# Attention-times-V in a fused transformer block: 16 tokens x 8 key offsets on the partitions, N=16 indicator sums, weights re-laid out through DRAM

## The chip, the cores and the metric

One core of a Trainium2 chip. The metric is the device time of the whole kernel in microseconds (us); the state of an execution (fast or slow) comes from its time and clock. PE is the tensor engine, DVE the vector engine, ACT the scalar engine, POOL the GpSimd engine; SP is the engine that issues the DMAs. "The Trainium skill" is the set of notes on the chip that is cited by page title.

## The reference, cut to what matters

A transformer block with conditioned layer norms: attention with 32 heads of 16 over eight dilated keys per token, then a gated FFN. 2,048 tokens of 512 features, bf16.

```python
W, dil = (8, 2)
idx = pos[:, None] - (jnp.arange(W) * dil)[None, :]     # keys s, s-2, ..., s-14
mask = idx >= 0
...
attn = _softmax(logits, axis=-1)                        # [head, token, 8]
o = jnp.einsum('bhsw,bhswd->bhsd', attn, vg)            # the AV product
...
x = x + ga * _A_ref(h, A_wqkv, A_wo)
h = _layernorm(x, axis=-1) * (1 + cb) + sb
x = x + gb * _B_ref(h, B_w1, B_w3, B_w2)
```

## The kernel before: the parts that matter

The program lists operations with dependences and priorities; a list scheduler with fixed cost guesses lays them out on the engines before the kernel is built, and semaphores are put in afterwards. So every change of the graph can change the order everywhere. There are 16 token tiles of 128 tokens, in four chunks of four. Per tile, attention forms q*k for eight offsets on DVE (128x4096), sums it over the head dimension on PE (32 matmuls of N=32), takes a softmax, multiplies V by it on DVE (128x4096) and sums over the offsets on PE:

```python
# V of the eight offsets, token s on partition s, offset w in the free dimension: one DMA
p.dma(lambda: vv.at[:], bass.AP(v_dram, T * P * D, [[D, P], [-2 * D, W], [1, D]]), ...)
def av(e):   # DVE: in place, attention weights straight from SBUF
    a_w = bass.AP(ve.at[0], 0, [[W * H, P], [H, W], [0, DH], [1, H]])
    v_w = bass.AP(vv.at, 0, [[W * D, P], [D, W], [H, DH], [1, H]])
    return e.tensor_tensor(v_w, v_w, a_w, ALU.mult)
def acc(e):  # PE: transposing sum over the 8 offsets, 4 feature blocks x 8 offsets, N = 128
    for ft in range(KT):
        for w in range(W):
            ins = e.matmul(b[:, ft * P:(ft + 1) * P], vv.at[:, w, ft * P:(ft + 1) * P], ident[:],
                           start=(w == 0), stop=(w == W - 1))
```

Token tile 0 has keys before the start of the sequence. It is handled by zeroing two buffers on POOL, by eight partial products and by seven small memsets:

```python
p.op("pool", lambda e: e.memset(vpq0.at[:], 0.0), 3600, -7e5, w=[vpq0])     # 128x4096
p.op("pool", lambda e: e.memset(vvsh0.at[:], 0.0), 3600, -7e5, w=[vvsh0])   # 128x4096
```

Of the kernel before, what the change touches and what calls it, by code (L numbers as in the profile page):

```python
# [7 lines left out]
ACT = mybir.ActivationFunctionType  # L8
# [3 lines left out]
P = 128  # L12
# [10 lines left out]
NCH = S // 512  # L23
EPS = 1e-5
# [36 lines left out]
class Op:  # L61
    __slots__ = ("eng", "fn", "cost", "pr", "deps", "vals", "n", "start", "end", "seen", "pos", "dma", "bytes",
                 "waits", "inc", "clock", "raw", "prev")

    def __init__(self, eng, fn, cost, pr):
        self.eng, self.fn, self.cost, self.pr = eng, fn, cost, pr
        self.deps = {}
        self.vals = []
        self.prev = []
        self.end = None  # L70
        self.dma = False
        self.bytes = 0
        self.inc = None


class Program:
# [37 lines left out]
    def dma(self, out, in_, pr, nbytes, r=(), w=(), part=(), after=(), eng="sp", cost=450):  # L114
# [8 lines left out]
        return self.op(eng, fn, cost, pr, r=r, w=w, part=part, after=after, dma=nbytes)  # L123
# [83 lines left out]
    def synchronize(self):  # L207
        known = {e: {} for e in ENGINES}
        waited = set()
        for o in self.placed:  # L210
            e = o.eng
            need = {}
            for d, true in list(o.deps.items()) + [(d, False) for d in o.prev]:
                if d.dma:
                    need[("dma", d.n)] = d
# [7 lines left out]
            for key, d in todo:  # L223
# [5 lines left out]
                for k, x in d.clock.items():  # L229
                    if have.get(k, 0) < x:  # L230
                        have[k] = x
# [5 lines left out]
        count = {e: 0 for e in ENGINES}  # L237
        for o in self.placed:
            if o.dma:
                o.inc = (self.ctx.enter_context(self.nc.semaphore(f"d{o.n}")), 16, 16)  # L240
# [47 lines left out]
def _build(p, A_x, A_wqkv, A_wo, B_w1, B_w3, B_w2, c, w_mod, out):  # L288
# [15 lines left out]
    kT = sb([P, KT, S], bf, "kT")  # L304
# [4 lines left out]
    vshb = [sb([P, W, D], bf, f"vsh{i}") for i in range(3)]  # L309
    pqb = [sb([P, W, KT, P], bf, f"pq{i}") for i in range(2)]  # L310
    osb = [sb([P, D], bf, f"o{i}") for i in range(2)]
    atb = [sb([P, W, H], bf, f"attn{i}") for i in range(2)]
    exb = [sb([P, W, H], f32, f"ex{i}") for i in range(2)]
# [3 lines left out]
    csb = sb([P, KT, P], bf, "csb")  # L317
    ident = sb([P, P], bf, "ident")
    E_sb = sb([P, KT, H], bf, "E")
    ones = sb([P, P], bf, "ones")  # L320
    cst = sb([P, 2], f32, "cst")
# [24 lines left out]
    wm_s = [at([P, KT, 1024], bf, f"wm_s{i}", 12288 * i) for i in range(2)]  # L346
    wm_g = [at([P, KT, 512], bf, f"wm_g{i}", 12288 * i + 8192) for i in range(2)]

    v_dram = nc.dram_tensor("v_scratch_dram", (S, D), bf)
# [13 lines left out]
    smpool = Pool("sm", [(atb[i], exb[i], i) for i in range(2)])  # L363
    otpool = Pool("ot", otb)
# [17 lines left out]
    vpq0 = Val("pq", pqpool)  # L382
    vvsh0 = Val("vsh", vshpool)
# [13 lines left out]
    p.op("pool", lambda e: e.memset(vpq0.at[:], 0.0), 3600, -7e5, w=[vpq0])  # L397
    p.op("pool", lambda e: e.memset(vvsh0.at[:], 0.0), 3600, -7e5, w=[vvsh0])
# [5 lines left out]
    vx = [Val(f"x{T}") for T in range(NT)]  # L404
    for T in range(4):
# [144 lines left out]
    def proj_qk(cch, kind, vh, pr):  # L550
        dstv = Val("q", qpool) if kind == 0 else Val("k")
        for ft in range(KT):
# [10 lines left out]
            def ev(e, ft=ft, vp=vp):  # L563
                if kind == 0:
                    return e.activation(dstv.at[:, ft, :], bank(vp), ACT.Copy, scale=SCALE)
                return e.activation(kT[:, ft, 512 * cch:512 * cch + 512], bank(vp), ACT.Copy)
# [4 lines left out]
    def proj_v(T, vh, pr):  # L571
# [19 lines left out]
        p.dma(v_dram[T * P:(T + 1) * P, :], lambda: vt.at[:], pr, 131072, r=[vt], w=[vd], cost=400)  # L591
# [5 lines left out]
    def attention(T, pr):  # L597
        cch = T // 4
        tt = T % 4
        ks = [vk[cch]] + ([vk[cch - 1]] if tt == 0 and T else [])  # L600
        if T == 0:
            vp = vpq0
            for w in range(W):
                def prod(e, w=w):
                    n = P - 2 * w
                    in0 = bass.AP(vq[0].at, 2 * w, [[KT * 512, P], [512, KT], [1, n]])
                    in1 = bass.AP(kT, 0, [[KT * S, P], [S, KT], [1, n]])
                    o = bass.AP(vp.at, w * KT * P + 2 * w, [[W * KT * P, P], [P, KT], [1, n]])
                    return e.tensor_tensor(o, in0, in1, ALU.mult)

                p.op("dve", prod, 400, pr, r=[vq[0]] + ks + ([vp] if w == 0 else []), part=[vp])
        else:
            vp = Val("pq", pqpool)

            def prod(e):
                in0 = bass.AP(vq[cch].at, tt * P, [[KT * 512, P], [0, W], [512, KT], [1, P]])
# [188 lines left out]
```

## Time and profile before

| | before |
|---|---|
| median | 295.06 us of 3 runs; 295.28 of 4 beside the changed kernel |
| span of the profiled execution | 295.4 us (a run of 297.19, slower than the median) |
| first QKV matmul | 16.47 us |
| first FFN matmul | 103.30 us |
| from there to the end | 192.1 us |

Busy time by engine (page, first part): us, share of the span, instructions.

```profile
PE 262.3 (89%) x2120; PEld 144.8 (49%) x2152; DVE 216.9 (73%) x369; ACT 134.5 (46%) x228; POOL 32.2 (11%) x60
```

The groups of the AV product (page, groups by line): partitions x elements, type, count | busy us, mean ns of one | idle just before. L665 is the DVE product, L674 the sums of N=128 on PE, L627 the logit sums of N=32.

```profile
L665 DVE TENSOR_TENSOR sb_vsh<-sb_vsh,sb_attn 128x4096 bf16<-128x4096 bf16 x16 | 36.5, 2284 | 0.0
...
L674 PE MATMUL pall<-sb_ident,sb_vsh 128*128 128x128 bf16 x512 | 31.2, 219 | 1.0 <-DVE sb_vsh L665 1.0
...
L627 PE MATMUL pall<-sb_E,sb_pq 128*128 128x32 bf16 x512 | 15.0, 177 | 2.0 <-DVE sb_pq L618 1.6
```

The two sums have equally many matmuls and weight loads, and busy time 31.2 against 15.0 us. (The mean of one matmul overlaps with its neighbours: divide busy time by the count.)

The table by stretches, cut at the first FFN matmul. Columns: stretch and length, then busy us (instructions) for PE, weight load, DVE, ACT, POOL; then granted clock, DMA share, GB/s.

```profile
core 0: us, PE busy (x) PEld busy (x) DVE busy (x) ACT busy (x) POOL busy (x), PEclk, DMA share, GB/s
0.00:103.30 103.30, 80.44 (x869) 48.95 (x881) 84.22 (x147) 50.59 (x86) 20.88 (x38) 0.95 0.74 233
103.30:295.40 192.10, 181.84 (x1251) 95.85 (x1272) 132.69 (x223) 83.90 (x143) 11.30 (x22) 0.98 0.16 52
```

In the second stretch PE is busy 95% of the time. In the first, DVE and PE are both at about 80%. The chain of waits is the work that ended last, followed back step by step. The chain over the whole span, and one burst of 32 AV sums in it:

```profile
PE 69%; DVE 21%; ACT 4%; issue 2%; POOL 2%; DMA 1%; DVEq 0%
...
110.34 1.79 PE pall L674 x32
```

DMA issues (page, last part): KB each and median us from issue to landing.

```profile
sb_vsh<-v_scratch_dram SPq DMA_DIRECT2D x15, 1024.0 KB, 5.1
...
out_dram<-sb_o SPq DMA_DIRECT2D x16, 128.0 KB, 1.7
```

### The profile page before, as it was taken

The page shows a single profiled execution, that of the slowest core. Times are in us where ns is not written, and L with a number is a line of the kernel's source. Part 1 is how long each engine was busy: PE and PEld are TensorE (multiplying, and loading weights), DVE is VectorE, ACT ScalarE, POOL GpSimd, SP SyncE. Part 2 cuts the span into 40 slices and gives each one's busy share as a digit, 9 for nine tenths or more (in the row PEclk, how much of TensorE's full clock was granted, in tenths as well). Part 3 has the DMA queues.
Part 4 walks back from the last instruction along what each step waited for, and adds up shares of the span by engine and source line. Part 5 has one row for each costly group of instructions (what it writes and reads, how often), then busy time and mean ns, then how long its engine had stood idle before and what let it go on. Part 6 is the DMA issues. An engine that isn't in the chain of part 4 may idle for free.

```text
span 295.4 us, 5127 instructions
## 1 busy us (share of the span) xinstructions
PE 262.3 (89%) x2120; PEld 144.8 (49%) x2152; DVE 216.9 (73%) x369; ACT 134.5 (46%) x228; POOL 32.2 (11%) x60
## 2 busy tenths in 40 slices
PE   0479996699999699999999999699999989999796
PEld 0324645357757345556545647355546634444342
DVE  4763988968999969989648997977588851366611
ACT  2146751654643645677105564140564570376500
POOL 8610001010311110010000010103100000000000
PEclk9999998599999979999999999799999999999999
DMA  5999994267726814124410040333000001100001
GB/s 180 360 287 359 335 294 163 87 204 215 241 85 197 254 50 145 43 100 143 161 36 20 2 142 11 133 81 118 18 2 1 2 0 36 38 0 0 0 20 53
DMA packets 34255, 34.10 MB, mean 115 GB/s; under 512 B 1775, under 2 KB 33207, under 8 KB 34231
## 3 DMA queue, kind: packets, MB, share of 16 engines
q1 hardware_dynamic: 34231, 33.77, 36.1%
q8 instruction: 17, 0.28, 0.4%
q14 instruction: 7, 0.06, 0.1%
HBM read 29.57 MB, written 4.19 MB: 114 GB/s over the span
## 4 chain that ended last, share of the span: by engine, by line
PE 69%; DVE 21%; ACT 4%; issue 2%; POOL 2%; DMA 1%; DVEq 0%
PE pall L702 27%; PE pall L726 17%; PE pall L558 9%; PE pall L674 6%; DVE sb_vsh L665 5%; PE pall L577 4%; DVE sb_pq L618 3%; ACT sb_h L531 3%; DVE sb_th L712 3%; PE pall L686 3%; PE pall L523 2%; PE pall L627 2%; DVE sb_st L493 2%; DVE sb_hh L715 2%; DVE sb_csT L443 1%
## 5 line engine op out<-in xcount | busy, mean ns | idle before, releaser
L702 PE MATMUL pall<-sb_h,sb_w 128*128 128x512 bf16 x435 | 99.7, 383 | 2.5 <-ACT sb_h L531 1.6
L702 PEld LDWEIGHTS pall<-sb_h,sb_w 128*128 128x128 bf16 x448 | 43.6, 99 | 52.9 <-issue 2.3
L726 PE MATMUL pall<-sb_w,sb_hh 128*128 128x512 bf16 x218 | 50.7, 387 | 5.8 <-DVE sb_hh L715 5.3
L712 DVE SCALAR_TENSOR_TENSOR sb_th<-sb_th,pall 128x512 bf16<-128x512 bf16 x56 | 37.8, 683 | 21.7 <-ACT sb_ub L710 21.3
L708 ACT ACTIVATE sb_th<-pall 128x512 bf16<-128x512 f32 x56 | 33.5, 597 | 33.9 <-PE pall L702 33.9
L710 ACT ACTIVATE sb_ub<-pall 128x512 bf16<-128x512 f32 x56 | 33.5, 598 | 28.7 <-PE pall L702 28.7
L726 PEld LDWEIGHTS pall<-sb_w,sb_hh 128*128 128x128 bf16 x224 | 22.1, 100 | 32.8 <-DVE sb_hh L715 6.1
L558 PE MATMUL pall<-sb_h,sb_wqkv 128*128 128x512 bf16 x123 | 32.5, 422 | 5.2 <-ACT sb_h L531 4.6
L665 DVE TENSOR_TENSOR sb_vsh<-sb_vsh,sb_attn 128x4096 bf16<-128x4096 bf16 x16 | 36.5, 2284 | 0.0
L618 DVE TENSOR_TENSOR sb_pq<-sb_q,sb_kT 128x4096 bf16<-128x4096 bf16 x15 | 34.2, 2284 | 1.9 <-PE pall L627 1.9
L531 ACT ACTIVATE sb_h<-pall,sb_modc 128x512 bf16<-128x512 bf16 x32 | 22.4, 778 | 23.1 <-PE pall L523 23.1
L674 PE MATMUL pall<-sb_ident,sb_vsh 128*128 128x128 bf16 x512 | 31.2, 219 | 1.0 <-DVE sb_vsh L665 1.0
L732 DVE TENSOR_TENSOR sb_o<-pall,sb_x 128x512 bf16<-128x512 f32 x16 | 11.1, 691 | 28.3 <-PE pall L726 28.2
L674 PEld LDWEIGHTS pall<-sb_ident,sb_vsh 128*128 128x128 bf16 x512 | 29.5, 98 | 4.3 <-ACT sb_v L587 1.0
L500 POOL TENSOR_TENSOR sb_rs<-sb_mv,sb_cst 128x1 f32<-128x1 f32 (+1 forms) x23 | 7.8, 343 | 205.8 <-DVE sb_mv L494 205.7
L493 DVE BATCH_NORM_STATS2 sb_st<-sb_x 128x6 f32<-128x512 bf16 x32 | 23.3, 839 | 3.0 <-DMA sb_x<-in_A_x_dram 2.9
L558 PEld LDWEIGHTS pall<-sb_h,sb_wqkv 128*128 128x128 bf16 x128 | 13.1, 107 | 22.4 <-issue 6.2
L715 DVE TENSOR_TENSOR sb_hh<-sb_th,sb_ub 128x512 bf16<-128x512 bf16 x56 | 22.9, 416 | 0.7
L680 ACT ACTIVATE sb_ot<-pall 128x512 bf16<-128x512 f32 x16 | 9.6, 598 | 27.0 <-PE pall L674 26.9
L627 PE MATMUL pall<-sb_E,sb_pq 128*128 128x32 bf16 x512 | 15.0, 177 | 2.0 <-DVE sb_pq L618 1.6
L686 PE MATMUL pall<-sb_wo,sb_ot 128*128 128x512 bf16 x61 | 16.1, 379 | 0.7 <-ACT sb_ot L680 0.5
L627 PEld LDWEIGHTS pall<-sb_E,sb_pq 128*128 128x128 bf16 x512 | 14.6, 96 | 4.3 <-DVE sb_pq L618 1.7
(52 smaller groups left out, 188.4 us busy)
## 6 DMA issues: line engine op xcount, KB each, us to landing
sb_vsh<-v_scratch_dram SPq DMA_DIRECT2D x15, 1024.0 KB, 5.1
sb_wm_s<-in_w_mod_dram SPq DMA_DIRECT2D x2, 1024.0 KB, 8.9
sb_w<-in_B_w_dram SPq DMA_DIRECT2D x4, 512.0 KB, 10.1
v_scratch_dram<-sb_v SPq DMA_DIRECT2D x16, 128.0 KB, 5.4
out_dram<-sb_o SPq DMA_DIRECT2D x16, 128.0 KB, 1.7
sb_w<-in_B_w_dram SPq DMA_DIRECT2D x1, 1792.0 KB, 11.5
sb_wqkv<-in_A_wqkv_dram SPq DMA_DIRECT2D x3, 512.0 KB, 8.0
sb_x<-in_A_x_dram SPq DMA_DIRECT2D x3, 512.0 KB, 9.5
```

What stands on the lines that cost most here:

```text
L493: p.op("dve", lambda e: e.bn_stats(st[:, i, :], x_sb[:, T, :]), 670, pr, r=[vx[T]], w=[vs])
L531: return e.activation(vh.at[:, ft, :], b[:, j * 512:(j + 1) * 512], ACT.Identity, bias=modc[:, 8 * which + ft:8 * which + ft + 1], scale=m ...
L558: ins = e.matmul(bank(vp), wqkv[:, t, col:col + P], vh.at[:, t, :], start=(t == 0), stop=(t == KT - 1))
L618: return e.tensor_tensor(vp.at[:], in0, in1, ALU.mult)
L627: ins = e.matmul(b[:, w * H:(w + 1) * H], vp.at[:, w, ft, :], E_sb[:, ft, :], start=(ft == 0), stop=(ft == KT - 1))
L665: return e.tensor_tensor(v_w, v_w, a_w, ALU.mult)
L674: ins = e.matmul(b[:, ft * P:(ft + 1) * P], vv.at[:, w, ft * P:(ft + 1) * P], ident[:], start=(w == 0), stop=(w == W - 1))
L702: ins = e.matmul(bank(vp), wt[:, t, fi * P:(fi + 1) * P], vh.at[:, t, :], start=(t == 0), stop=(t == KT - 1))
L708: p.op("act", lambda e: e.activation(vt.at[0][:], bank(vgp), ACT.Tanh, scale=0.5), 540, pr, r=[vgp], w=[vt])
L710: p.op("act", lambda e: e.activation(vt.at[1][:], bank(vup), ACT.Copy), 540, pr, r=[vup], w=[vu], part=[vt])
L712: p.op("dve", lambda e: e.scalar_tensor_tensor(vt.at[0][:], vt.at[0][:], 1.0, bank(vgp), op0=ALU.add, op1=ALU.mult), 700, pr, r=[vgp, vt], ...
L726: ins = e.matmul(bank(vz), vhh[(cch, fi)].at[:, tt * P:(tt + 1) * P], w2[:, fi, :], start=(fi == 0), stop=(fi == NF - 1))
```

## The change

Put 16 tokens times 8 offsets on the 128 partitions and eight groups of 16 tokens in the free dimension. A sum over the offsets is then a sum over groups of eight partitions, which a matmul against a 128x16 indicator does, with N=16 instead of N=128 and no accumulation. V can be read from DRAM in this layout. The attention weights come out of softmax with tokens on the partitions and must be moved: they are stored to DRAM and loaded back. K and V also get 16 rows of zeros in front, so that tile 0 needs one mask and neither of the POOL memsets.

```diff
-            p.dma(lambda: vv.at[:], bass.AP(v_dram, T * P * D, [[D, P], [-2 * D, W], [1, D]]), pr - 1, 1048576,
-                  r=[vv_dram[T], vv_dram[T - 1]], w=[vv], cost=450)
+        p.dma(a_dram[T * P:(T + 1) * P, :], lambda: ve.at[0].rearrange("p w h -> p (w h)"), pr, 65536, r=[va, ve], w=[vad], cost=400)
+        p.dma(lambda: val.at[:], bass.AP(a_dram, T * P * W * H, [[H, P], [16 * W * H, 8], [1, H]]), pr, 65536 * 4, r=[vad],
+              w=[val], cost=400)
+        for g in range(8):
+            p.dma(lambda g=g: vv.at[:, g, :], bass.AP(v_dram, (PAD + T * P + 16 * g) * D, [[D, 16], [-DIL * D, W], [1, D]]),
+                  pr - 1, 131072, r=[vv_dram[T]] + ([vv_dram[T - 1]] if T else [vvpad]), part=[vv], cost=450, group=grp)
...
-            for ft in range(KT):
-                for w in range(W):
-                    ins = e.matmul(b[:, ft * P:(ft + 1) * P], vv.at[:, w, ft * P:(ft + 1) * P], ident[:], start=(w == 0),
-                                   stop=(w == W - 1))
+            for g in range(8):
+                for ft in range(KT):
+                    ins = e.matmul(b[:, ft * P + 16 * g:ft * P + 16 * g + 16], vv.at[:, g, ft * P:(ft + 1) * P], ind[:],
+                                   start=True, stop=True)
...
-    p.op("pool", lambda e: e.memset(vpq0.at[:], 0.0), 3600, -7e5, w=[vpq0])
-    p.op("pool", lambda e: e.memset(vvsh0.at[:], 0.0), 3600, -7e5, w=[vvsh0])
...  (padding of kT and v_dram, one product and one mask for tile 0)
```

More of the change, by code (lines that the diff above doesn't have):

```diff
@@ L23 @@
 NCH = S // 512
+PAD = 16
 EPS = 1e-5
@@ L62 @@
     __slots__ = ("eng", "fn", "cost", "pr", "deps", "vals", "n", "start", "end", "seen", "pos", "dma", "bytes",
-                 "waits", "inc", "clock", "raw", "prev")
+                 "waits", "inc", "clock", "prev", "group")
     def __init__(self, eng, fn, cost, pr):
@@ L73, in __init__ @@
         self.inc = None
+        self.group = [self]
 class Program:
@@ L112, in op, with dma @@
         return o
-    def dma(self, out, in_, pr, nbytes, r=(), w=(), part=(), after=(), eng="sp", cost=450):
+    def dma(self, out, in_, pr, nbytes, r=(), w=(), part=(), after=(), eng="sp", cost=450, group=None):
         nc = self.nc
@@ L121, in fn @@
                 return e.dma_start(a, b)
-        return self.op(eng, fn, cost, pr, r=r, w=w, part=part, after=after, dma=nbytes)
+        o = self.op(eng, fn, cost, pr, r=r, w=w, part=part, after=after, dma=nbytes)
+        if group is not None:
+            group.append(o)
+            o.group = group
+        return o
     def schedule(self):
@@ L214, in synchronize @@
                 if d.dma:
-                    need[("dma", d.n)] = d
+                    need[("dma", d.group[0].n)] = d
                 elif d.eng != e or (true and e not in ("pe", "sp")):
@@ L228, in synchronize @@
                 waited.add(d)
-                for k, x in d.clock.items():
-                    if have.get(k, 0) < x:
-                        have[k] = x
+                for m in d.group:
+                    for k, x in m.clock.items():
+                        if have.get(k, 0) < x:
+                            have[k] = x
                 have[key] = max(have.get(key, 0), level)
@@ L237, in synchronize @@
         count = {e: 0 for e in ENGINES}
+        dsem = {}
         for o in self.placed:
             if o.dma:
-                o.inc = (self.ctx.enter_context(self.nc.semaphore(f"d{o.n}")), 16, 16)
+                first = o.group[0]
+                if first.n not in dsem:
+                    dsem[first.n] = self.ctx.enter_context(self.nc.semaphore(f"d{first.n}"))
+                o.inc = (dsem[first.n], 16, 16 * len(o.group))
             elif o in waited:
@@ L303, in _build @@
     w2 = sb([P, NF, D], bf, "w2")
-    kT = sb([P, KT, S], bf, "kT")
+    kT = sb([P, KT, PAD + S], bf, "kT")
     qb = [sb([P, KT, 512], bf, f"q{i}") for i in range(3)]
@@ L308, in _build @@
     vb = [sb([P, D], bf, f"v{i}") for i in range(4)]
-    vshb = [sb([P, W, D], bf, f"vsh{i}") for i in range(3)]
+    vshb = [sb([P, 8, D], bf, f"vsh{i}") for i in range(3)]
     pqb = [sb([P, W, KT, P], bf, f"pq{i}") for i in range(2)]
@@ L312, in _build @@
     atb = [sb([P, W, H], bf, f"attn{i}") for i in range(2)]
+    alb = [sb([P, 8, H], bf, f"al{i}") for i in range(3)]
     exb = [sb([P, W, H], f32, f"ex{i}") for i in range(2)]
@@ L316, in _build @@
     gb_bc = sb([P, D], bf, "gb_bc")
-    csb = sb([P, KT, P], bf, "csb")
     ident = sb([P, P], bf, "ident")
@@ L320, in _build @@
     ones = sb([P, P], bf, "ones")
+    ind = sb([P, 16], bf, "ind")
+    mask0 = sb([P, W], f32, "mask0")
     cst = sb([P, 2], f32, "cst")
@@ L346, in _build @@
     wm_s = [at([P, KT, 1024], bf, f"wm_s{i}", 12288 * i) for i in range(2)]
+    csb = at([P, KT, P], bf, "csb", 24576)
+    zrow = at([PAD, D], bf, "zrow", 25600)
     wm_g = [at([P, KT, 512], bf, f"wm_g{i}", 12288 * i + 8192) for i in range(2)]
-    v_dram = nc.dram_tensor("v_scratch_dram", (S, D), bf)
+    v_dram = nc.dram_tensor("v_scratch_dram", (PAD + S, D), bf)
+    a_dram = nc.dram_tensor("a_scratch_dram", (S, W * H), bf)
     PALL = ctx.enter_context(nc.psum_tensor("pall", [P, 8 * 512], f32))
@@ L363, in _build @@
     smpool = Pool("sm", [(atb[i], exb[i], i) for i in range(2)])
+    alpool = Pool("al", alb)
     otpool = Pool("ot", otb)
@@ L381, in _build @@
     vident = Val("ident")
-    vpq0 = Val("pq", pqpool)
-    vvsh0 = Val("vsh", vshpool)
     p.op("pool", lambda e: e.memset(ones[:], 1.0), 150, -9e5, w=[vc])
@@ L396, in _build @@
                                            pattern=[[-128, KT], [16, H]], channel_multiplier=-1), 320, -8e5, w=[vE])
-    p.op("pool", lambda e: e.memset(vpq0.at[:], 0.0), 3600, -7e5, w=[vpq0])
-    p.op("pool", lambda e: e.memset(vvsh0.at[:], 0.0), 3600, -7e5, w=[vvsh0])
+    vind = Val("ind")
+    p.op("pool", lambda e: e.memset(ind[:], 1.0), 100, -7e5, w=[vind])
+    p.op("pool", lambda e: e.affine_select(out=ind[:], in_=ind[:], compare_op=ALU.is_ge, fill=0.0, base=0,
+                                           pattern=[[-8, 16]], channel_multiplier=1), 160, -7e5, w=[vind])
+    p.op("pool", lambda e: e.affine_select(out=ind[:], in_=ind[:], compare_op=ALU.is_ge, fill=0.0, base=7,
+                                           pattern=[[8, 16]], channel_multiplier=-1), 160, -7e5, w=[vind])
+    vmask0 = Val("mask0")
+    p.op("pool", lambda e: e.memset(mask0[:], 1.0), 100, -7e5, w=[vmask0])
+    p.op("pool", lambda e: e.affine_select(out=mask0[:], in_=mask0[:], compare_op=ALU.is_ge, fill=0.0, base=0,
+                                           pattern=[[-DIL, W]], channel_multiplier=1), 160, -7e5, w=[vmask0])
+    vkpad, vzrow, vvpad = Val("kpad"), Val("zrow"), Val("vpad")
+    p.op("dve", lambda e: e.memset(zrow[:], 0.0), 300, -200, w=[vzrow])
+    p.op("dve", lambda e: e.memset(kT[:, :, 0:PAD], 0.0), 120, -200, w=[vkpad])
     wm_view = w_mod.rearrange("(t p) n -> p t n", p=P)
@@ L404, in _build @@
     vx = [Val(f"x{T}") for T in range(NT)]
+    vpad_dma = p.dma(v_dram[0:PAD, :], zrow[:], 500, 16384, r=[vzrow], w=[vvpad])
     for T in range(4):
@@ L565, in ev @@
                     return e.activation(dstv.at[:, ft, :], bank(vp), ACT.Copy, scale=SCALE)
-                return e.activation(kT[:, ft, 512 * cch:512 * cch + 512], bank(vp), ACT.Copy)
+                return e.activation(kT[:, ft, PAD + 512 * cch:PAD + 512 * cch + 512], bank(vp), ACT.Copy)
             p.op("act", ev, 540, pr + ft, r=[vp], part=[dstv])
@@ L590, in proj_v @@
         vd = Val("vd")
-        p.dma(v_dram[T * P:(T + 1) * P, :], lambda: vt.at[:], pr, 131072, r=[vt], w=[vd], cost=400)
+        p.dma(v_dram[PAD + T * P:PAD + (T + 1) * P, :], lambda: vt.at[:], pr, 131072, r=[vt], w=[vd], cost=400)
         vv_dram[T] = vd
@@ L599, in attention, with prod @@
         tt = T % 4
-        ks = [vk[cch]] + ([vk[cch - 1]] if tt == 0 and T else [])
-        if T == 0:
-            vp = vpq0
-            for w in range(W):
-                def prod(e, w=w):
-                    n = P - 2 * w
-                    in0 = bass.AP(vq[0].at, 2 * w, [[KT * 512, P], [512, KT], [1, n]])
-                    in1 = bass.AP(kT, 0, [[KT * S, P], [S, KT], [1, n]])
-                    o = bass.AP(vp.at, w * KT * P + 2 * w, [[W * KT * P, P], [P, KT], [1, n]])
-                    return e.tensor_tensor(o, in0, in1, ALU.mult)
-                p.op("dve", prod, 400, pr, r=[vq[0]] + ks + ([vp] if w == 0 else []), part=[vp])
-        else:
-            vp = Val("pq", pqpool)
-            def prod(e):
-                in0 = bass.AP(vq[cch].at, tt * P, [[KT * 512, P], [0, W], [512, KT], [1, P]])
-                in1 = bass.AP(kT, T * P, [[KT * S, P], [-DIL, W], [S, KT], [1, P]])
-                return e.tensor_tensor(vp.at[:], in0, in1, ALU.mult)
-            p.op("dve", prod, 2290, pr, r=[vq[cch]] + ks, w=[vp])
+        ks = [vk[cch]] + ([vk[cch - 1]] if tt == 0 and T else []) + ([vkpad] if T == 0 else [])
+        vp = Val("pq", pqpool)
+        def prod(e):
+            in0 = bass.AP(vq[cch].at, tt * P, [[KT * 512, P], [0, W], [512, KT], [1, P]])
+            in1 = bass.AP(kT, PAD + T * P, [[KT * (PAD + S), P], [-DIL, W], [PAD + S, KT], [1, P]])
+            return e.tensor_tensor(vp.at[:], in0, in1, ALU.mult)
+        p.op("dve", prod, 2290, pr, r=[vq[cch]] + ks, w=[vp])
         vl = Val("ps_l", psum)
@@ L642, in attention @@
         if T == 0:
-            for w in range(1, W):
-                p.op("dve", lambda e, w=w: e.memset(ve.at[1][0:2 * w, w, :], 0.0), 70, pr, part=[ve], r=[ve] if w == 1 else [])
+            p.op("dve", lambda e: e.tensor_tensor(ve.at[1][:], ve.at[1][:], bass.AP(mask0, 0, [[W, P], [1, W], [0, H]]),
+                                                  ALU.mult), 430, pr, r=[vmask0], w=[ve])
         p.op("dve", lambda e: e.tensor_reduce(ssum[:, ve.at[2], :], ve.at[1].rearrange("p w h -> p h w"), AX.X, ALU.add), 600,
@@ L651, in attention @@
                                               ALU.mult), 430, pr, r=[vr, ve], w=[va])
-        if T == 0:
-            vv = vvsh0
-            for w in range(W):
-                p.dma(lambda w=w: vv.at[2 * w:P, w, :], bass.AP(v_dram, 0, [[D, P - 2 * w], [1, D]]), pr - 1, 131072,
-                      r=[vv_dram[0]] + ([vv] if w == 0 else []), part=[vv])
-        else:
-            vv = Val("vsh", vshpool)
-            p.dma(lambda: vv.at[:], bass.AP(v_dram, T * P * D, [[D, P], [-2 * D, W], [1, D]]), pr - 1, 1048576,
-                  r=[vv_dram[T], vv_dram[T - 1]], w=[vv], cost=450)
+        vad, val = Val("ad"), Val("al", alpool)
+        p.dma(a_dram[T * P:(T + 1) * P, :], lambda: ve.at[0].rearrange("p w h -> p (w h)"), pr, 65536, r=[va, ve], w=[vad], cost=400)
+        p.dma(lambda: val.at[:], bass.AP(a_dram, T * P * W * H, [[H, P], [16 * W * H, 8], [1, H]]), pr, 65536 * 4, r=[vad],
+              w=[val], cost=400)
+        vv = Val("vsh", vshpool)
+        grp = []
+        for g in range(8):
+            p.dma(lambda g=g: vv.at[:, g, :], bass.AP(v_dram, (PAD + T * P + 16 * g) * D, [[D, 16], [-DIL * D, W], [1, D]]),
+                  pr - 1, 131072, r=[vv_dram[T]] + ([vv_dram[T - 1]] if T else [vvpad]), part=[vv], cost=450, group=grp)
         def av(e):
-            a_w = bass.AP(ve.at[0], 0, [[W * H, P], [H, W], [0, DH], [1, H]])
-            v_w = bass.AP(vv.at, 0, [[W * D, P], [D, W], [H, DH], [1, H]])
+            a_w = bass.AP(val.at, 0, [[8 * H, P], [H, 8], [0, DH], [1, H]])
+            v_w = bass.AP(vv.at, 0, [[8 * D, P], [D, 8], [H, DH], [1, H]])
             return e.tensor_tensor(v_w, v_w, a_w, ALU.mult)
-        p.op("dve", av, 2290, pr, r=[va, ve], w=[vv])
+        p.op("dve", av, 2290, pr, r=[val], w=[vv])
         vo = Val("ps_o", psum)
@@ L671, in acc @@
             b = bank(vo)
-            for ft in range(KT):
-                for w in range(W):
-                    ins = e.matmul(b[:, ft * P:(ft + 1) * P], vv.at[:, w, ft * P:(ft + 1) * P], ident[:], start=(w == 0),
-                                   stop=(w == W - 1))
+            for g in range(8):
+                for ft in range(KT):
+                    ins = e.matmul(b[:, ft * P + 16 * g:ft * P + 16 * g + 16], vv.at[:, g, ft * P:(ft + 1) * P], ind[:],
+                                   start=True, stop=True)
             return ins
-        p.op("pe", acc, 1850, pr, r=[vv, vident], w=[vo])
+        p.op("pe", acc, 980, pr, r=[vv, vind], w=[vo])
         vt = Val("ot", otpool)
@@ L757, in _build @@
             gate(1, TT * 0.6)
-            region_prev = list(wm_users)
+            region_prev = list(wm_users) + [vpad_dma]
             for pool in (hhpool, tmppool):
```

## The prediction

> **What bounds the kernel now.** Two stages. Until about 103 us VectorE (DVE) sets the pace: the table by stretches has DVE busy 31.6 of 35.0 us (27 to 62) and 38.4 of 41.3 (62 to 103.3), and the first FFN matmul at 103.3 us follows the layer norm of token tile 3, which is late in DVE's order. From there to the end (192 us) TensorE (PE) is the bound: busy 38.3 of 38.7, 32.1 of 35.0 and 47.1 of 48.0 us in three of its stretches, with DVE a second limit between 158 and 193 (32.0 of 35.0). The chain of waits agrees: PE 69%, DVE 21%.
>
> **What the change removes.** The chain shows each burst of 32 AV sums (N=128) as 1.79 us, 56 ns a matmul; the bursts of 32 logit sums (N=32, as many weight loads) take 0.79 us, 25 ns each. The Trainium skill, "TensorE: Matmul & The Clock Gate", section "Back-to-back issue gap", gives one floor of about 25 ns for N from 1 to 64 and 134 cycles for N=128; the trace agrees. So N=16 should cost what N=32 does, 0.8 us a burst and not an eighth of 1.79. Saved: 1.0 us a tile, 16 us of PE in all. Tile 0's eight partial products and seven memsets become one product and one mask: about 0.7 us less DVE. Two 3.5 us POOL memsets go; nothing waited for them.
>
> **What it adds.** Per tile a 64 KB store and a reload as 1024 pieces of 64 B, in series between softmax and the AV product; the V read becomes eight DMAs. Stores of 128 KB land in 1.7 us (DMA issues), and SP spends 0.33 us per such issue: about 3 us more SP time a tile, and an estimated 4 to 7 us more latency from softmax to AV. The AV product keeps its shape, 2.28 us.
>
> **What of it is critical.** Before the first FFN matmul PE's saving is worth almost nothing. DVE's order there changes: with durations from the trace I count 67 us of DVE work from the first QK product to the normalization of tile 3, against 65 before (71 us of wall time), and tile 4's AV product in that stretch has its weights reloaded with little to spare. I expect the first FFN matmul at 103 to 107 us. After it, the order leaves 168.8 us of PE work where there were 178.8, counted alike; eleven instead of ten AV sums are left. So 10 us come off the bound stage. DVE has 5.6 us more work before the second chunk's last gate product, so I expect 1 to 3 us of new PE waits between 155 and 200 us, more where SP's in-order queue holds a reload behind a V read that waits for a buffer.
>
> **Predicted:** 288 us (2.4% less), 8 in 10 between 282 and 295. Chances: faster by over 2% 0.56, within 2% 0.39, slower by over 2% 0.05.
>
> **Right if:** AV sums take about 25 ns each, 0.8 us a burst; AV product still 2.28 us; PE busy time lower by 14 to 17 us; first FFN matmul at 103 to 107 us; from there to the end 182 to 186 us. **Wrong if:** AV sums over 35 ns; AV products idle over 1 us each for the reload; reload landing in over 8 us; first FFN matmul later than 109 us.
>
> **What would make it wrong.** Head-of-line blocking on SP, which waits in order for each store to land before it issues the reload: if most AV products wait for it, DVE stalls, gate products come late, and PE's saving turns into waits. The other way: if the rearranged order starts FFN work earlier, the gain is nearer the full 16 us.

## The result, and the profile after

284.24 us median of 4 runs (283.52 to 286.08) against 295.28 of before. The ratio is 0.9625, 95% interval 0.9551 to 0.9699. Ratios here are the mean time of one kernel's fast runs over that of the other's of the same rounds, so not quite the ratio of the medians. A later repeat (e9 below) gave 0.9591. The time lies in the predicted range, 3.8 us under the predicted value.

Busy time by engine after (page, first part):

```profile
PE 249.3 (88%) x2152; PEld 127.8 (45%) x2152; DVE 213.6 (76%) x358; ACT 134.7 (48%) x228; POOL 27.8 (10%) x63
```

PE lost 13.0 us of busy time, less than the 14 to 17 predicted. This understates it: before, 32 of 2,152 matmul records are missing from the trace. Between e1 below, with wide sums, and after, where no record is missing, PE's busy time differs by 16.4 us (265.7 against 249.3).

The same groups after (L680 is the DVE product, L689 the AV sums, L642 the logit sums):

```profile
L680 DVE TENSOR_TENSOR sb_vsh<-sb_vsh,sb_al 128x4096 bf16<-128x4096 bf16 x16 | 36.5, 2284 | 4.2 <-DMA sb_al<-a_scratch_dram 4.2
...
L689 PE MATMUL pall<-sb_ind,sb_vsh 128*128 128x16 bf16 x512 | 15.2, 169 | 3.7 <-DVE sb_vsh L680 1.9
...
L642 PE MATMUL pall<-sb_E,sb_pq 128*128 128x32 bf16 x512 | 14.8, 176 | 3.7 <-DVE sb_pq L633 3.7
```

AV sums of N=16 are busy 15.2 us, logit sums of N=32 14.8: the narrower sum is no cheaper, as predicted. In the chain of waits most bursts take 0.78 to 0.80 us against 1.79 (two take 0.96 and 0.97, and one of before 1.96). The DVE product keeps its 2.28 us. The chain of after, and one burst:

```profile
PE 73%; DVE 13%; ACT 4%; DMA 3%; SPq 3%; POOL 2%; issue 1%
...
65.29 0.79 PE pall L689 x32
```

The stretches, cut at the first FFN matmul:

```profile
0.00:100.67 100.67, 76.26 (x908) 42.78 (x908) 80.76 (x136) 50.00 (x85) 18.70 (x41) 0.94 0.78 231
100.67:281.80 181.13, 173.05 (x1244) 84.98 (x1244) 132.83 (x223) 84.74 (x144) 9.12 (x22) 0.99 0.27 72
```

The first stretch is 2.6 us shorter, the second 11.0. (These are single executions, and the profiled one of before was a slow-ish run, so 13.6 us here stands against 11.0 between the medians.) Counting the matmuls that the order leaves after the first FFN matmul, at the spacings of the trace (0.2155 us for N=512, 56 ns for 128, 25 ns for 16 and 32), gives 178.8 us before and 168.8 after: the second stretch fell by what PE's work fell, plus 1 us. (Before's granted clock dips to a mean of 0.93 between 175 and 200 us, after's stays at 1.00; that may be part of the extra 1 us.)

What was added, in the DMA issues of after:

```profile
sb_vsh<-v_scratch_dram SPq DMA_DIRECT2D x128, 128.0 KB, 2.7
...
a_scratch_dram<-sb_attn SPq DMA_DIRECT2D x16, 64.0 KB, 2.1
sb_al<-a_scratch_dram SPq DMA_DIRECT2D x16, 64.0 KB, 2.5
```

Store and reload land in 2.1 + 2.5 = 4.6 us. And what the AV product waits for the reload, in the view of waits (us in total, times, longest):

```profile
DVE sb_vsh L680 <- DMA sb_al<-a_scratch_dram: 4.2, 4, 2.3
```

Four of sixteen products wait, 4.2 us in all. The chain of after passes through two of these waits, at 83 and at 98 us: each time SP issues a row of V reads before it gets to the reload (SPq is SP's issuing, 3% of the span, and DMA another 3%). The prediction had named such a queue as a risk; e5 tests what the waits cost.

Not predicted at all was the start. DVE's timeline, before:

```profile
4.03 1.27 DVE L442 TENSOR_SCALAR sb_csT_bf<-sb_csT_bf 128x4 bf16<-128x4 bf16 x1
5.33 3.69 DVE L443 CAST sb_csT<-sb_csT_bf 128x4 f32<-128x4 bf16 x1
5.46 3.56 DVE L493 BATCH_NORM_STATS2 sb_st<-sb_x 128x6 f32<-128x512 bf16 x2
```

POOL's timeline in the same time, before:

```profile
1.76 3.51 POOL L397 MEMSET sb_pq<- 128x4096 bf16 x1
...
5.49 3.51 POOL L398 MEMSET sb_vsh<- 128x4096 bf16 x1
...
9.33 0.33 POOL L500 TENSOR_TENSOR sb_rs<-sb_mv,sb_cst 128x1 f32<-128x1 f32 x2
```

And DVE's timeline after:

```profile
4.00 0.17 DVE L469 TENSOR_SCALAR sb_csT_bf<-sb_csT_bf 128x4 bf16<-128x4 bf16 x1
4.21 0.17 DVE L470 CAST sb_csT<-sb_csT_bf 128x4 f32<-128x4 bf16 x1
4.28 1.28 DVE L520 BATCH_NORM_STATS2 sb_st<-sb_x 128x6 f32<-128x512 bf16 x2
```

Before, a DVE cast of four elements "took" 3.69 us and ended together with a POOL memset of 3.51 us; after, the same cast takes 0.17 us. The first QKV matmul starts at 14.31 us, 2.2 us earlier than before.

### The profile page after: what moved, and what is told of

It reads as the page before. It is cut to its first block, busy times and chain, and to the rows that moved or that the text cites. A ratio compares the mean times of both kernels' runs of the same rounds, so it can differ in the third digit from the quotient of the medians.

```text
span 281.8 us, 5292 instructions
## 1 busy us (share of the span) xinstructions
PE 249.3 (88%) x2152; PEld 127.8 (45%) x2152; DVE 213.6 (76%) x358; ACT 134.7 (48%) x228; POOL 27.8 (10%) x63
## 4 chain that ended last, share of the span: by engine, by line
PE 73%; DVE 13%; ACT 4%; DMA 3%; SPq 3%; POOL 2%; issue 1%
PE pall L717 29%; PE pall L741 17%; PE pall L585 12%; DVE sb_vsh L680 5%; PE pall L604 4%; PE pall L701 3%; ACT sb_h L558 3%; PE pall L689 3%; SPq L123 3%; PE pall L642 2%; DMA sb_al<-a_scratch_dram 2%; PE pall L550 2%; POOL sb_rs L529 1%; DVE sb_th L727 1%; DVE sb_st L520 1%
## 5 line engine op out<-in xcount | busy, mean ns | idle before, releaser
L717 PE MATMUL pall<-sb_h,sb_w 128*128 128x512 bf16 x448 | 103.0, 386 | 2.8 <-ACT sb_h L558 2.8
L741 PE MATMUL pall<-sb_w,sb_hh 128*128 128x512 bf16 x224 | 49.7, 379 | 2.3 <-DVE sb_hh L730 2.3
L633 DVE TENSOR_TENSOR sb_pq<-sb_q,sb_kT 128x4096 bf16<-128x4096 bf16 x16 | 36.3, 2278 | 5.0 <-PE pall L642 3.3
L680 DVE TENSOR_TENSOR sb_vsh<-sb_vsh,sb_al 128x4096 bf16<-128x4096 bf16 x16 | 36.5, 2284 | 4.2 <-DMA sb_al<-a_scratch_dram 4.2
L585 PE MATMUL pall<-sb_h,sb_wqkv 128*128 128x512 bf16 x128 | 33.4, 422 | 5.4 <-ACT sb_h L558 4.7
L527 POOL TENSOR_TENSOR sb_rs<-sb_mv,sb_cst 128x1 f32<-128x1 f32 (+1 forms) x23 | 9.5, 417 | 203.8 <-DVE sb_mv L521 203.8
L520 DVE BATCH_NORM_STATS2 sb_st<-sb_x 128x6 f32<-128x512 bf16 x32 | 21.2, 680 | 4.6 <-DMA sb_x<-in_A_x_dram 4.6
L550 PE MATMUL pall<-sb_ident,sb_xn 128*128 128x128 bf16 x128 | 11.7, 236 | 10.1 <-DVE sb_xn L536 8.2
L689 PE MATMUL pall<-sb_ind,sb_vsh 128*128 128x16 bf16 x512 | 15.2, 169 | 3.7 <-DVE sb_vsh L680 1.9
L689 PEld LDWEIGHTS pall<-sb_ind,sb_vsh 128*128 128x128 bf16 x512 | 14.5, 96 | 8.5 <-DVE sb_vsh L680 3.0
L642 PE MATMUL pall<-sb_E,sb_pq 128*128 128x32 bf16 x512 | 14.8, 176 | 3.7 <-DVE sb_pq L633 3.7
L701 PE MATMUL pall<-sb_wo,sb_ot 128*128 128x512 bf16 x64 | 16.5, 379 | 1.6 <-ACT sb_ot L695 1.6
```

The costliest lines, as they stand in the source:

```text
L520: p.op("dve", lambda e: e.bn_stats(st[:, i, :], x_sb[:, T, :]), 670, pr, r=[vx[T]], w=[vs])
L585: ins = e.matmul(bank(vp), wqkv[:, t, col:col + P], vh.at[:, t, :], start=(t == 0), stop=(t == KT - 1))
L633: return e.tensor_tensor(vp.at[:], in0, in1, ALU.mult)
L689: ins = e.matmul(b[:, ft * P + 16 * g:ft * P + 16 * g + 16], vv.at[:, g, ft * P:(ft + 1) * P], ind[:], start=True, stop=True)
L701: ins = e.matmul(bank(vy), vt.at[:, ft, :], wo[:, ft, :], start=(ft == 0), stop=(ft == KT - 1))
L717: ins = e.matmul(bank(vp), wt[:, t, fi * P:(fi + 1) * P], vh.at[:, t, :], start=(t == 0), stop=(t == KT - 1))
```

## The experiments

All ran beside the kernel before on the same chip. e1 to e4, e5 to e8, e9 to e11 and e12 were four jobs on four chips, so ratios to before are what compares across jobs. Each profile is one execution; after, e5 and e9, which share one order, start the FFN at 100.5 to 101.5 us, so differences below 1 us in these columns mean nothing. "PE work left" is the count just described. The medians are of all runs, one slow one in e4, e9 and e11 and two in e8 among them; the ratios use fast runs alone. The job of e5 to e8 had no control run of after, and their executions show a mean granted clock of 0.942 to 0.958, where after and e9's fast runs show 0.958 to 0.970. In the profiles of e5, e6 and e7 the clock dips between 200 and 240 us (mean 0.91, 0.96 and 0.96 there, against 1.00 in after and e9). So part of what separates these runs from after is this dip; what caused it is not known.

| run | median us | ratio to before (95%) | first QKV | first FFN | PE work left | FFN start to end |
|---|---|---|---|---|---|---|
| before | 295.3 | 1 | 16.5 | 103.3 | 178.8 | 192.1 |
| after | 284.2 | 0.9625 (0.9551 to 0.9699) | 14.3 | 100.7 | 168.8 | 181.1 |
| e1 N=128 sums | 297.4 | 1.0047 (0.9991 to 1.0103) | 14.2 | 104.8 | 179.9 | 191.0 |
| e2 N=64 sums | 286.2 | 0.9688 (0.9625 to 0.9752) | 14.1 | 101.9 | - | 181.6 |
| e3 padding alone | 294.6 | 0.9951 (0.9890 to 1.0012) | 14.1 | 96.8 | 180.4 | 194.1 |
| e4 memsets back | 288.7 | 0.9739 (0.9672 to 0.9805) | 18.1 (slow) | 106.6 (slow) | 168.8 | - |
| e5 no wait for reload | 285.9 | 0.9629 (0.9580 to 0.9679) | 14.2 | 100.5 | 168.8 | 183.5 |
| e6 one V read | 289.8 | 0.9781 (0.9717 to 0.9846) | 14.1 | 101.3 | 169.7 | 186.2 |
| e7 trip on ACT's queue | 291.4 | 0.9824 (0.9778 to 0.9870) | 14.1 | 98.9 | 176.5 | 191.1 |
| e8 SBUF to SBUF | 297.7 | 0.9958 (0.9880 to 1.0036) | - | - | 172.9 | - |
| e9 after again | 284.7 | 0.9591 (0.9555 to 0.9627) | 14.2 | 101.5 | 168.8 | 179.9 |
| e10 tiles 0-3 old | 291.6 | 0.9821 (0.9779 to 0.9862) | 14.2 | 97.4 | 171.3 | 192.5 |
| e11 tiles 0-5 old | 288.6 | 0.9700 (0.9652 to 0.9747) | 15.1 (slow) | 98.5 (slow) | 170.4 | - |
| e12 memsets later | 290.2 | 0.9778 (0.9723 to 0.9833) | 19.7 | 108.1 | 168.8 | 181.3 |

### e1: the sums wide again, everything else as after

The 16 indicator columns sit in a wider tile of zeros; a shifted slice of 128 columns makes the same sums with N=128. The order of the compute engines and of every DMA is that of the changed kernel; POOL has one more small memset at the start.

```diff
-    ind = sb([P, 16], bf, "ind")
+    ind = sb([P, 240], bf, "ind")          # ones pattern in columns 112..127, zeros elsewhere
...
-                    ins = e.matmul(b[:, ft * P + 16 * g:ft * P + 16 * g + 16], vv.at[:, g, ft * P:(ft + 1) * P], ind[:],
-                                   start=True, stop=True)
+                    ins = e.matmul(b[:, ft * P:ft * P + 128], vv.at[:, g, ft * P:(ft + 1) * P],
+                                   ind[:, 112 - 16 * g:240 - 16 * g], start=(g == 0), stop=(g == 7))
```

> The changed kernel with only the AV sums made 128 columns wide again (indicator shifted inside a wide zero tile, eight matmuls accumulate), every engine's order and every DMA unchanged. Theory A (the gain after the first FFN matmul is PE time, 1.0 us a tile): bursts of 32 sums take 1.8 us instead of 0.8, PE busy rises by 16 us, and 10 to 13 us of it come back in the time: 294 to 298 us. Rival B (the gain comes from the new order, the padding and the freed POOL): the time stays below 288 us although PE is busier.

Measured: 297.41 us, not faster than before at all. The sums' group and the stretches:

```profile
L690 PE MATMUL pall<-sb_ind,sb_vsh 128*128 128x128 bf16 x512 | 31.3, 219 | 2.7 <-DVE sb_vsh L681 1.9 <-DVE sb_x L707 0.8
```

```profile
0.00:104.79 104.79, 82.06 (x909) 48.36 (x909) 81.15 (x136) 49.82 (x85) 18.96 (x42) 0.93 0.77 224
104.79:295.80 191.01, 183.62 (x1244) 95.81 (x1244) 132.81 (x223) 84.73 (x144) 9.14 (x22) 0.99 0.25 67
```

The busy time of the sums is 31.3 us, before's 31.2, and the median is 13.2 us above that of after (two jobs; the ratios differ by 4.2%). So theory A holds: the narrow sums are the whole gain, and without them the change gains nothing that the interval can show. Against after, 9.9 us of the difference lie after the first FFN matmul and 4.1 before it (3.3 against e9).

### e2: sums 64 columns wide

The same code with slices of 64 columns and accumulation over four groups.

> The same with sums 64 columns wide. Theory A with the floor (one cost for 1 to 64 columns): bursts of 32 stay at 0.8 to 0.9 us and the time within 1.5 us of the changed kernel's. Rival (cost grows with the columns from 16 on, 25 ns at 16 and 56 ns at 128, so about 38 ns at 64): bursts of 1.2 us, time up by about 4 us.

```profile
L690 PE MATMUL pall<-sb_ind,sb_vsh 128*128 128x64 bf16 x512 | 17.8, 192 | 3.6 <-DVE sb_vsh L681 1.9 <-DVE sb_x L707 1.6
```

Busy 17.8 us against 15.2 with N=16. A burst in the chain is mostly 0.95 us, so 29.7 ns a matmul: neither the flat floor nor the 38 ns of the rival, but nearer the floor. The logit sums also accumulate over four matmuls and take 25 ns, so the accumulation is not what costs. The time is 2.0 us over after's median, a little above the 1.5 that theory A allowed, but the two intervals overlap. Going from 32 columns to 16 buys nothing; in the burst, though not clearly in the time, 64 already cost something.

### e3: the padding alone, on the kernel before

```diff
-    p.op("pool", lambda e: e.memset(vpq0.at[:], 0.0), 3600, -7e5, w=[vpq0])
-    p.op("pool", lambda e: e.memset(vvsh0.at[:], 0.0), 3600, -7e5, w=[vvsh0])
+    (16 zero rows before K and V; tile 0 like every tile, with one mask; AV layout and N=128 sums as before)
```

> The kernel before with only the padding part of the change: K and V padded, one product and one mask for token tile 0, no POOL memsets; AV layout and N=128 sums as before. Theory C (the two 3.5 us POOL memsets block DVE's small casts, 3.69 us for a cast that takes 0.17 us in the changed kernel): the cast takes 0.17 us, the first QKV matmul starts near 14.3 us instead of 16.5, time 2 to 3.5 us below before. Rival (as I predicted, nothing waited for the memsets): at most 0.7 us below before.

```profile
0.00:96.81 96.81, 79.32 (x816) 47.09 (x816) 77.24 (x135) 49.20 (x84) 12.92 (x38) 0.95 0.78 248
96.81:290.90 194.09, 183.09 (x1336) 97.85 (x1336) 136.38 (x223) 84.80 (x145) 9.46 (x22) 0.99 0.16 52
```

The cast takes 0.17 us and the first QKV matmul starts at 14.14 us, as theory C said. The first FFN matmul comes 6.5 us earlier than before in these profiles: beside the early start, tile 0 is cheaper and the order is new, with eight logit sums done by then instead of ten. The run does not separate these. But the time fell by only 1.1 us between the medians, ratio 0.9951 with an interval that includes 1: less than the 2 to 3.5 expected. 180.4 us of PE work remain after the early start where before had 178.8, and the second stretch takes 194.1 us instead of 192.1. An earlier first FFN matmul is not time saved one for one.

### e4: the two memsets back in the changed kernel

They write V buffers that are loaded much later, at the place in POOL's order where the kernel before had them. No other engine's order changes.

```diff
-    p.op("pool", lambda e: e.affine_select(out=E_sb[:], ...          # both of them
+    ms1 = p.op("pool", lambda e: e.memset(vshb[1][:], 0.0) and e.affine_select(out=E_sb[:], ...
+    ms2 = p.op("pool", lambda e: e.memset(vshb[2][:], 0.0) and e.affine_select(out=E_sb[:], ...
```

> The changed kernel with two POOL memsets of 128x4096 put back at the same place, into V buffers that are loaded much later; the order on every other engine is unchanged. Theory C: DVE's tensor_scalar and cast on 4 elements stretch to over 1 us and over 3 us, the first QKV matmul moves from 14.3 to 16.5 us or later, time 2 to 4 us above the changed kernel. Rival (the memsets were free): within 0.7 us of the changed kernel.

288.67 us, 1.2% over after by the ratios (3.4 us). Its interval is clear of e9's (0.9555 to 0.9627) but touches that of after's first measurement. The rival falls, less by the time than by the start of the first QKV matmul, 18.1 us: the memsets are not free. But theory C was not right about how. The profile is slow, so only the DVE and POOL instructions of its start are read here. Tensor_scalar stretched (1.32 us) while the cast, which slipped in between the two memsets, took 0.23 us. POOL's own queue did the rest: the first layer norm's additions for the reciprocal square root (L527) wait behind the memsets. DVE's own statistics (batch_norm_stats2) run beside the second memset at 0.66 to 0.68 us each, as in after: not every DVE instruction is held.

```profile
1.89 3.51 POOL L408 MEMSET sb_vsh<- 128x4096 bf16 x1
...
5.76 3.51 POOL L410 MEMSET sb_vsh<- 128x4096 bf16 x1
...
9.79 0.33 POOL L527 TENSOR_TENSOR sb_rs<-sb_mv,sb_cst 128x1 f32<-128x1 f32 x2
```

### e12: the memsets behind the layer norm in POOL's queue

To separate the two causes, the same memsets were placed after the fourth reciprocal square root, where POOL's queue holds up nothing needed for the first QKV matmul.

```diff
+            if which == 0 and T0 == 3:       # after this square root, on POOL
+                e.memset(vshb[1][:], 0.0)
+                e.memset(vshb[2][:], 0.0)
```

> The changed kernel with the same two POOL memsets as in the run e4_memsets, but placed on POOL behind the last reciprocal square root of the first layer norm, so that POOL's queue holds up nothing that the first QKV matmul needs; every other engine's order unchanged. What is left is whether a running POOL memset blocks DVE. If it does (the 3.69 us cast of the kernel before), DVE's normalization and casts between 9 and 16 us stretch by 1 to 3.5 us each and the first QKV matmul moves from 14.2 to 15.5 us or later, time up by 1.5 to 5 us. If e4's loss was POOL's own queue alone: the casts stay at 0.17 us, first QKV matmul near 14.2 us, time within 1 us of the changed kernel.

290.18 us. DVE, then POOL:

```profile
8.71 7.54 DVE L543 TENSOR_SCALAR sb_xn<-sb_x,sb_mv,sb_rs 128x512 bf16<-128x512 bf16 x2 [0.28 <-POOL sb_rs L530]
16.17 0.15 DVE L493 CAST sb_modc_bf<-pall 128x8 bf16<-128x8 f32 x1
```

```profile
9.15 3.51 POOL L532 MEMSET sb_vsh<- 128x4096 bf16 x1
12.60 3.51 POOL L533 MEMSET sb_vsh<- 128x4096 bf16 x1
```

Two DVE normalizations that take 0.93 us together in after take 7.54 us, and end with the second memset: the first, begun before the memsets, took 0.41 us and the other 7.02. So a running POOL memset does block a DVE tensor_scalar. The first QKV matmul moved to 19.67 us and the time rose by 1.6% by the ratios (4.5 us; 5.9 between the medians); from the first FFN matmul on the run takes 181.3 us, like after. This is what the Trainium skill says, "SBUF — State Buffer", section "Who interferes with whom": cast and tensor_scalar can, in the modes that use two ports, take the port pair that DVE shares with GpSimd, and whichever issues first holds it for its whole instruction. The prediction does not use this. Both causes are real: in the kernel before, DVE was blocked until 9.02 us, and POOL's second memset ended at 9.00 us too, so removing either alone might have gained little there. That was not run.

### e5: the AV product does not wait for the reload (wrong result)

```diff
-            a_w = bass.AP(val.at, 0, [[8 * H, P], [H, 8], [0, DH], [1, H]])
+            a_w = bass.AP(ga_bc, 0, [[D, P], [H, 8], [0, DH], [1, H]])      # a constant tile of the same shape
```

The dependence on the reload is dropped with the data; order and DMAs are unchanged.

> Wrong result on purpose. The changed kernel, every engine's order and every DMA unchanged, but the AV product multiplies by a constant tile and so does not wait for the reloaded attention weights (4.2 us of DVE waits in four places of the changed kernel's trace, 0.8 and 2.3 us of them in the chain). Theory D (the reload's latency costs what its waits show and little more): those waits vanish and the time falls by 1 to 4 us. Rival E (the wait hides behind other work): less than 0.8 us.

Ratio 0.9629, after had 0.9625 and 0.9591. The waits are gone from the trace and the time did not move by anything that the intervals can show. The dip of the clock could hide a gain, but PE's order is the same in after, e9 and e5, so each instruction can be set against the same one in the other traces. From 115 us to 227 us, past the last AV sum, e5 is 0.6 us ahead of after and 0.1 us ahead of e9; then the clock dips in e5 alone (0.78 between 220 and 230 us) and it falls 2.2 us behind after. Theory D falls, rival E holds: in this order the waits cost 0.6 us or less, though the chain of waits counts 3.1 us of them (0.8 and 2.3). A piece of the chain can vanish without the time falling by its length. The comparison with the reference called this result correct. Its tolerance therefore does not see the attention weights, and "correct" says little about the AV layout in any of these runs.

### e6, e7, e8: three other ways to move the data

e6 groups tokens as 8t + g. Eight rows of V are then one run of 8 KB, and a tile's V is one DMA.

```diff
-        for g in range(8):
-            p.dma(lambda g=g: vv.at[:, g, :], bass.AP(v_dram, (PAD + T * P + 16 * g) * D, [[D, 16], [-DIL * D, W], [1, D]]), ...
+        p.dma(lambda: vv.at[:].rearrange("p g d -> p (g d)"), bass.AP(v_dram, (PAD + T * P) * D, [[8 * D, 16], [-DIL * D, W], [1, 8 * D]]), ...
...
-                    ins = e.matmul(b[:, ft * P + 16 * g:ft * P + 16 * g + 16], vv.at[:, g, ft * P:(ft + 1) * P], ind[:],
+                    ins = e.matmul(b[:, ft * P + g:(ft + 1) * P:8], vv.at[:, g, ft * P:(ft + 1) * P], ind[:],
```

> Token tiles regrouped as token = 8t + g in place of 16g + t: the eight rows of a group are then one run of 8 KB and the whole V read is one DMA of 128 pieces; the store of the attention weights is permuted to match and the sums write every eighth column. Result stays correct. Theory F (the eight V issues of 0.6 us each on SP hold back the reloads): SP time a tile falls by about 4.5 us, the AV product's waits for the reload fall from 4.2 to under 2 us, time 1 to 4 us lower, 281 to 283. Rival: SP's issue time is off the chain, within 1 us of the changed kernel, or slower if sums into every eighth column take over 25 ns.

Slower than after by 1.6 to 2% (by the ratios), although the product's waits for the reload fell to 1.4 us, as theory F said. The sums into every eighth column cost the same, 15.3 us busy. SP's time for V fell from eight issues of 0.60 us to one of 0.56. The DMAs, though, land later:

```profile
sb_vsh<-v_scratch_dram SPq DMA_DIRECT2D x16, 1024.0 KB, 8.0
...
a_scratch_dram<-sb_attn SPq DMA_DIRECT2D x16, 64.0 KB, 3.6
```

V takes 8.0 us instead of 2.7 for each eighth (eight of them, issued over 4.8 us), the stores behind it 3.6 instead of 2.1, and DVE now waits 3.1 us for stores before it may reuse a buffer. The order changed as well, and the runs do not separate the two. Theory F's gain does not appear; whether less issue time alone would help after stays open, since it came here only with later landings.

e7 issues store and reload from ACT (`eng="act"` on the two DMAs, nothing else).

> The changed kernel with store and reload of the attention weights issued by ScalarE instead of SP, so that they do not queue behind V reads that wait for a buffer. Theory F: the AV waits for the reload fall below 2 us, time 1 to 3 us lower. Rival: ScalarE's own in-order queue takes the place of SP's (it spends about 0.4 us an issue and waits for each store to land), FFN evictions are held up, and the time rises by 2 us or more.

Slower by about 2%, with the waits of the product for the reload gone from the view of waits. It is the rival's outcome, but not clearly its mechanism. ACT's busy time (134.1 against 134.7 us in after) does not decide it, because issuing a DMA and waiting for a landing do not count as busy; the 32 issues take ACT 12.1 us in the trace. The order changed too: the scheduler starts the FFN at 98.9 us with 176.5 us of PE work left, 7.7 more than after, and PE waits 7.5 us for AV products where after waits 1.9. The run does not separate these. It shows again that an early start with more left over is no gain.

e8 goes from SBUF to SBUF in eight DMAs of 128 pieces of 64 B, on top of e6.

```diff
+            p.dma(lambda g=g: val.at[:, g, :], lambda g=g: bass.AP(ve.at[0], g * W * H, [[8 * W * H, 16], [H, W], [1, H]]), ...
```

> Like the run with one V read, but the weights go from SBUF to SBUF in eight DMAs of 128 pieces of 64 B, without the trip through DRAM: one landing instead of two in series. Theory D: latency from softmax to AV falls by about 2 us and the time is at or below that of the run with one V read. Rival F (issue time counts more than landings): eight issues of 0.4 to 0.6 us replace two, and the time is 1 us or more above it.

297.67 us, two of four runs and the profile slow; the two fast ones had 294.44 and 296.27. It is slower than e6, as rival F expected; in its (slow) profile eleven products wait 16.9 us for the reload, where in e6 two wait 1.4.

### e9, e10, e11: the old layout for the first tiles

e3 had started its FFN at 96.8 us and e1 at 104.8, so the trip seemed to cost 8 us before the first FFN matmul. e10 and e11 take the old AV layout for the first four or six tiles, with after as a control on the same chip (five rounds).

```diff
+        if T < 4:        # 6 in e11
+            (V read, product and N=128 sums of the kernel before)
+        else:
             (the changed kernel)
```

> The changed kernel itself, as the control for the two hybrids on the same chip: ratio to the kernel before 0.955 to 0.970, AV bursts 0.8 us, first FFN matmul at 100 to 102 us of the span.

> The changed kernel with token tiles 0 to 3, those that the first FFN matmul needs, in the old AV layout (no trip through DRAM, sums of 128 columns); tiles 4 to 15 in the new one. Theory G (before the first FFN matmul the DRAM trip and the order built around it cost about 8 us, 96.8 us with the padding alone against 104.8 us with the new layout and equally wide sums, while the narrow sums win back only 4): first FFN matmul at 96 to 99 us; 171.3 us of PE work are left after it where the changed kernel has 168.8, so the time is 0 to 3 us lower. Rival H (the start is set by DVE's and PE's work, and e3's early start was its order's luck): first FFN matmul at 100 us or later, time 1 to 3 us higher.

> The same with tiles 0 to 5 in the old layout, all six whose sums come before the first FFN matmul. Theory G: first FFN matmul at 96 to 98 us as with the padding alone, 170.4 us of PE work left after it, time 1 to 3 us below the changed kernel. Rival H: no earlier start, time 1 to 4 us higher.

Both start the FFN earlier, as theory G said (97.4 us in e10 against 101.5 in e9), and both are slower: 291.55 and 288.55 us against 284.70. What was won is lost twice after the start. The stretches of e10, then its longest PE wait after the first FFN matmul, then that group's wait in after:

```profile
0.00:97.43 97.43, 76.90 (x830) 46.16 (x843) 74.83 (x129) 49.37 (x84) 12.32 (x39) 0.93 0.76 233
97.43:289.90 192.47, 174.74 (x1288) 87.31 (x1310) 138.28 (x230) 85.03 (x145) 11.79 (x24) 0.97 0.26 68
```

```profile
PE pall L712 <- DVE sb_vsh L703: 8.6, 3, 5.2
```

```profile
PE pall L689 <- DVE sb_vsh L680: 1.9, 1, 1.9
```

e10 has 171.3 us of PE work left and takes 192.5 us for it; after takes 181.1 us for 168.8. PE waits 8.6 us for AV products where after waits 1.9, and DVE has 138.3 us of work in that stretch instead of 132.8. The order explains the direction: after has twelve logit sums done when the FFN starts, e10 ten and e11 eight, so more attention is left to be done beside the FFN. After the start the DVE product waits 6.3 us for the reload in e10, 3.3 in after, and e10's chain there passes through rows of issues on SP, V reads among them, ahead of two reloads (at 108 and 172 us). Its granted clock also dips, to a mean of 0.86 between 175 and 200 us. How much of the 21 us between 192.5 and 171.3 is which of these stays open. No version tried here beats after.

## Why the prediction was right or wrong, point by point

- **N=16 costs what N=32 does.** Right: mostly 0.78 to 0.80 us a burst, 15.2 us busy against 14.8. e2 shows that the flat part ends before 64.
- **The AV product keeps 2.28 us.** Right: 2,284 ns in both.
- **10 us come off the second stretch; 182 to 186 us from the first FFN matmul.** Right in mechanism and nearly in size: 11.0 us, 181.1 us. e1 attributes it, with 191.0 us when only the width of the sums is put back.
- **"Before the first FFN matmul PE's saving is worth almost nothing."** This term was mis-sized. Five sums of 1.0 us each come before that matmul, and e1 measures 4.1 us against after, 3.3 against e9. The step behind it failed too: "VectorE (DVE) sets the pace". In the prediction's own two stretches, 27 to 103.3 us, DVE is busy 70.0 us and PE 67.1, and the chain runs through PE for 37.0 us and through DVE for 26.4. An engine that is busiest is not therefore the only bound.
- **"Two 3.5 us POOL memsets go; nothing waited for them."** Wrong. Before, a 0.17 us cast waited 3.69 us, and the first QKV matmul started 2.2 us later. By the ratios e4 costs 3.4 us when the memsets return, e12 4.5 us when they run where DVE needs the port. In time, though, their removal with the padding is worth only about 1 us to the kernel before, not clear of noise (e3). The view of waits had shown no waiter because a blocked instruction counts as busy; the mean of 3,690 ns for a four-element cast was on view.
- **First FFN matmul at 103 to 107 us.** Wrong, 100.7. The two terms above are large enough for it: with memsets in DVE's way it is 108.1 (e12), with wide sums 104.8 (e1).
- **4 to 7 us more latency from softmax to AV, and 1 to 3 us of new PE waits.** The latency is right, 4.6 us for the two landings, but PE waits after the first FFN matmul did not grow in sum (7.8 us before, 7.9 after): the waits for gate products fell from 5.3 to 2.3 us and 1.9 us of waits for AV products appeared. e5, set against after instruction by instruction, puts the cost of the waits for the reload at 0.6 us or less.
- **"About 3 us more SP time a tile".** Too small: an issue in a row of eight takes SP 0.60 us (median), 4.8 us for V. What that costs was not isolated: e6 removes it, but lands V later.

So the total came out 3.8 us high: two terms of the first stretch were set to zero, and the new PE waits of the second did not add up. That the predicted value came so close is in part luck, since the parts forecast, taken at their middles (105 and 184 us of the span), sum to more than the total of 288. e1 and e3 give the balance: padding and memsets about -1 us, new layout with its DRAM trip about +3 (neither clear of noise), narrow sums about -13.

## What to carry to other kernels

A narrow moving operand paid here from 128 columns (56 ns a matmul) to 64 (29.7) and a little more to 32 (25), and then stopped (25 at 16); cost it by a group of the same width in the same trace. Before calling work free because nobody is seen to wait for it, look for instructions of other engines that are longer than their size allows while it runs. And an earlier start of the last stage is no gain by itself: count the work that the order leaves after it, on the engine that bounds it and on the engines that feed it.

## What the Trainium skill lacked or had wrong

- "TensorE: Matmul & The Clock Gate", section "Back-to-back issue gap": its table gives about 25 ns for any N from 1 to 64. The trace agrees at 16 and 32 (0.79 us for 32 matmuls), but at 64 a burst takes 0.95 us, 29.7 ns each (e2). The formula above that table gives 29.2 ns. The same section puts the sustained spacing at about 81 ns for N=128 and 131 for N=512, and says that the formula counts too little at small N and too much at large. Here real streams run at 56 ns (1.79 us for 32) and 215.5 ns, which is what the formula gives (55.8 and 215.8).
- "SBUF — State Buffer", section "Who interferes with whom": right as far as tested, and it would have warned of the wrong step. It speaks of one blocking instruction, and says that the first to issue wins; in e12 one DVE instruction was held across two POOL memsets in a row, 7.02 us for 0.41 us of work, and in before a cast recorded as starting at 5.33 us was held by a memset that starts at 5.49, while a short POOL select ran between the memsets. It does not say how such a block looks in a profile: as busy time of the blocked engine, not as a wait.
- "DMA: Bandwidth & Descriptors": its rules say what a DMA needs to run fast, but none gives for trn2 the time that an issue takes SP (a table about trn3 has a cycle count for "previous generations", without a chip or a time): here 0.33 us for single 128 KB stores to the output, 0.60 us in rows of eight. And 1 MB in 128 pieces of 8 KB landed in 8.0 us (e6) where 1,024 pieces of 1 KB had taken 5.1 (before); the runs do not show why.
